# Four release points a period for held-back DMAs, W1's turned loads one user sooner, the first row squares ahead of the last gradient product

## The chip, the core and the metric

The kernel runs on one core of one Trainium2 chip. A core has five engines with an instruction stream each: TensorE (PE in the profile; weight loads are listed apart as PEld), VectorE (DVE), ScalarE (ACT), GpSimd (POOL) and SyncE (SP). Each works through its stream in order. DMAs are issued by SP, ACT or POOL, each into a queue of its own ("SPq" is SP's); 16 DMA engines move the data. A DMA whose operands are not ready makes its issuing engine wait, and all that stands behind it in that stream.

The metric is the device time of one execution in microseconds, as the median of several runs.

## The reference

One training step's forward and backward pass of a gated mix of two layers over a sequence of 2048 rows with 448 columns (bf16): a state space layer, written as a long convolution, and a dense layer with a squared ReLU.

```
def _A_ref(u, A_re, A_im, B_re, B_im, C_re, C_im, log_dt, Dskip):
    ...
    P = jnp.exp(logdA[:, :, None] * l[None, None, :])
    K = jnp.einsum("dn,dnl,dn->dl", Cc, P, dB).real
    ...                      # y = causal convolution of u with K, by FFT
    return y + u * Dskip
def _B_ref(x, w1, b1, w2, b2):
    h = jnp.einsum("bsd,df->bsf", x, w1) + b1
    r = jnp.where(h > zero, h, zero)
    return jnp.einsum("bsf,fd->bsd", r * r, w2) + b2
g = sigmoid((u * gate_w).sum(-1, keepdims=True))
out = g * a + (1 - g) * b
```

The kernel returns `out` and the gradients of `sum(out * grad_out)` by the 14 inputs other than `B_x` (the dense layer's input is `u`). Sizes: D = 448, N = 256 states, F = 1792 hidden columns, w1 448 x 1792, w2 1792 x 448.

## The kernel before

Three stages follow each other. Up to about 230 us the inputs are loaded and taken through the FFT's forward passes, and a scheduler orders the instructions. From then on the order is the program's own (`tc.manual_schedule()`, line 981): each engine runs what the Python code emits, in that sequence. This second stage, to about 625 us, interleaves two strands that have nothing to do with each other's data. From there the inverse passes and the parameter gradients close the run.

**Strand one, the convolution kernel and its gradient.** 14 chunks of 32 columns (NCH), one a period. `PERIOD` (line 1286) lists what a period does as tokens, and `token` (line 1289) carries each out. What matters here: YS puts seeds into the table Y on DVE (`seeds_y`, L1055), Y0 to Y4 build its levels on DVE (`step_y`, L1014, L1015, L1017), KM multiplies the tables on PE (`kgen`, L1078), LY issues four transposing loads of Y on SP (`load_yt`, L1102, "turned" below; they go into four tiles in R), Z0 to Z3 use these tiles on PE one period later (`back_z`, L1140), with an ACT copy each (L1146); P0 and P1 are products on DVE (L1155, L1157), S sums them on PE (L1172), X0 to X2 build the other table (L1004, L1005, L1007), FY0 to FY2 spread fields on ACT (L1040 to L1047). The seeds of the next period overwrite Y, so L1055 waits until the four turned loads have read it.

**Strand two, the dense layer.** `dense` (line 923) is a generator of small steps, and D in the list runs as many of them as their costs allow (`D_`, line 945). It consists of `first_layer`, `second_layer` and two `project` passes:

- `second_layer` (line 820) goes over 14 blocks j of 128 hidden columns. `grad_h` forms the gradient of the hidden rows on PE (L661, L664), ACT copies it into one of three tiles `dhs[j % 3]` (L784; they lie in P, F and R), `gates` multiplies it with r on DVE (L789). The function `go` then loads the r rows of block j + 3 (`load_r`, L772 or, in two halves, L775) and stores the block to `dhT_d` (L794). The block is also turned on PE (`turn`, L688, copy L689), multiplied by the input rows (`mul_2`, L697, copied out by L805), and the product turned back for storing (`turn_back`: L808, L811, L813, L814). `turn_w2` (L765, L766) prepares w2 blocks.
- `project(0, w2n)` (line 881) computes the layer's output from the squared hidden rows, `project(1, w1T)` its input gradient from `dhT_d`. Each goes over 8 row groups n of 256 rows with two halves x: 14 matmuls into a bank (L901), a copy (L904). The rows of a group come by `load_rows2(n)` (L877) into a ring of four places. In the first pass ACT squares them in place (L889): group 0 before the loop, group n + 1 while n is multiplied. After a group its place is free, and the load of group n + 4 is asked for; with it, for the first seven groups, one seventh of W1 turned (`load_w1t`, L921, a transposing load into `w1T`, which the second pass needs whole).

**Held-back DMAs.** SP's queue is in order, and the turned loads take it long. So the stores and loads above are not emitted where they are asked for. `defer` (line 633) puts them on a list `held`, and `release` (line 639) emits the list. In a period that happens at LY (behind its four loads) and at the token R, between the eighth D and FY1. Two other places force it: `force` in `hidden` and `grad_h`, where a tile is about to be reused, and a test at the head of `project`'s loop.

```
def defer(i, f):
    if hold:
        held.append((i, f))
...
elif o == "LY" and new:
    YTs[c] = [load_yt(j) for j in range(4)]
    release()
```

Of the kernel before, what the change touches and what calls it, by code (L numbers as in the profile page):

```python
# [12 lines left out]
ACT = mybir.ActivationFunctionType  # L13
# [6 lines left out]
P = 128  # L20
L, D, N, F = 2048, 448, 256, 1792
# [298 lines left out]
def kernel(ctx, tc, A_u, A_A_re, A_A_im, A_B_re, A_B_im, A_C_re, A_C_im, A_log_dt, A_Dskip,  # L320
# [4 lines left out]
    V, S, G_, T_ = nc.vector, nc.scalar, nc.gpsimd, nc.tensor  # L325
# [307 lines left out]
# [3 lines that stand above are left out]
        else:  # L636
            f()

    def release():
        while held:  # L640
            held.pop(0)[1]()
# [43 lines left out]
    def turn(j, th, src, f):  # L685
        ps = K.ps(BK["t"], [P, 8, P], bf16)
        for tt in range(8):
            T_.transpose(ps[:, tt, :], src[:, (8 * th + tt) * P:(8 * th + tt + 1) * P], ident[:])  # L688
        S.activation(hn[j % 2][:, 8 * th:8 * th + 8, :], ps[:], f)  # L689

    def mul_rows(j, th, rhs, w):
        acc[1] = th == 0
        if th == 0:
            acc[0] = K.ps(BK["a"], [P, 512])
        ps = acc[0]
        for t in range(8 * th, 8 * th + 8):
            T_.matmul(ps[:, 0:w], lhsT=hn[j % 2][:, t, :], rhs=rhs[:, t, :], start=(t == 0), stop=(t == LT - 1))  # L697
        return ps
# [14 lines left out]
    HP = FT // 2  # L713
# [47 lines left out]
    def turn_w2(j):  # L761
        ps = K.ps(BK["t"], [P, DT, P], bf16)
        for dt in range(DT):
            for h in range(1 if dt < 3 else 2):
                T_.transpose(ps[64 * h:64 * h + DSZ[dt], dt], w2b[j % 2][:, dt * P:dt * P + DSZ[dt]], ident[:], tile_position=(0, 64 * h))  # L765
        S.copy(w2T[j % 2], ps[:])  # L766
        if j + 2 < FT:
            load_w2(j + 2)

    def load_r(j):  # L770
        if j % 3 > 0:
            nc.sync.dma_start(rt[j % 3 - 1], rows_of(rT_d, j))  # L772
        else:
            for h in range(2):
                nc.sync.dma_start(r3[0][h], bass.AP(tensor=rT_d, offset=j * P * L + 1024 * h, ap=[[L, P], [1, 1024]]))  # L775

    def grad_h(j, half):

        force(j - 3)
        pss = wide(half, w2T[j % 2], lambda lb: dbt[lb])  # L780
        dh = dhs[j % 3]
        for k in range(2):
            lb = 2 * half + k
            S.mul(dh[:, 512 * lb:512 * lb + 512], pss[k][:], 2.0)  # L784

        def gate():
            force(j - 3)
            d = dh[:, 1024 * half:1024 * half + 1024]
            V.tensor_tensor(out=d, in0=d, in1=r3[j % 3][half], op=ALU.mult)  # L789
            if half == 1:  # L790
                def go():
                    if j + 3 < FT:
                        load_r(j + 3)
                    nc.sync.dma_start(rows_of(dhT_d, j), dh)  # L794
                defer(j, go)
        pend.append(gate)

    def gates():
        while pend:
            pend.pop(0)()  # L800

    def mul_2(j, th):
        ps = mul_rows(j, th, Un, D + 1)
        if th == 1:
            S.copy(dw1r[:, j % 2, 0:D + 1], ps[:, 0:D + 1])  # L805
# [14 lines left out]
    def second_layer():  # L820

        release()
        for j in range(acc.get("r", 0), 3):
            load_r(j)
        for half in range(2):
            turn_w2(half)
        for half in range(2):
            gates()
            grad_h(0, half)
            yield  # L830
        for j in range(FT):
            gates()
            if j in (3, 5, 7, 9):
                k0, k1 = (4 * (j // 2) - 4, min(4 * (j // 2), FT))
                defer(j, lambda k0=k0, k1=k1: nc.sync.dma_start(w2n[:, k0:k1], bass.AP(tensor=B_w2.tensor, offset=B_w2.offset + k0 * P * D, ap=[[D, P], [P * D, k1 - k0], [1, D]])))
            if j == FT - 1:
                load_rows2(0)
            if j + 1 < FT:
                grad_h(j + 1, 0)
            turn(j, 0, dhs[j % 3], ACT.Copy)  # L840
            yield
            if j > 0:
                mul_2(j - 1, 1)
            if j + 2 < FT:
                turn_w2(j + 2)
            yield
            gates()
            if j + 1 < FT:
                grad_h(j + 1, 1)
            turn(j, 1, dhs[j % 3], ACT.Copy)  # L850
            yield
            mul_2(j, 0)
            if j > 0:
                turn_back(j - 1)
            yield
        mul_2(FT - 1, 1)
        yield
        turn_back(FT - 1)
        load_rows2(1)
        defer(98, lambda: load_rows2(2))  # L860
        defer(99, lambda: load_rows2(3))

    PO = [0, 4, 1, 5, 2, 6, 3, 7]

    def user(n):

        return 12 if n == 15 else n - 4

    def slot_of(n):

        return pring[0 if n == 15 else n % 4]

    def load_rows2(n):
        bs = slot_of(n)
        m = FT // len(bs)
        for i, b in enumerate(bs):
            nc.sync.dma_start(b, bass.AP(tensor=rT_d if n < 8 else dhT_d, offset=256 * PO[n % 8] + i * m * P * L, ap=[[L, P], [P * L, m], [1, 256]]))  # L877
# [3 lines left out]
    def project(w, ws):  # L881

        nonlocal nbk

        def square(n, x):
            if w == 0:
                for b in slot_of(n):
                    v = b[:, :, P * x:P * x + P]
                    S.activation(v, v, ACT.Square)  # L889
        for x in range(2):  # L890
            square(0, x)
        for n in range(8):
            for x in range(2):
                t = 2 * PO[n] + x
                if any(98 <= k <= 100 + user(n + 8 * w + (w == 0 and n < 7)) for k, f in held):
                    release()
                nbk += 1
                ps = K.ps(BK["p"][nbk % len(BK["p"])], [P, 512])
                src = [b[:, j] for b in slot_of(n + 8 * w) for j in range(FT // len(slot_of(n + 8 * w)))]
                for j in range(FT):  # L900
                    T_.matmul(ps[:, 0:D], lhsT=src[j][:, P * x:P * x + P], rhs=ws[:, j, :], start=(j == 0), stop=(j == FT - 1))  # L901
                    if j == HP - 1:
                        yield
                S.copy(br[w][:, t], ps[:, 0:D])  # L904
                if n < 7:
                    square(n + 1, x)
                if x == 0:
                    gates()
                elif w == 0:
                    pend.append(lambda v=br[0][:, t - 1:t + 1]: V.tensor_tensor(out=v, in0=v, in1=b2_bc[:].unsqueeze(1).to_broadcast([P, 2, D]), op=ALU.add))  # L910
                if x == 1:
                    i = n + 8 * w
                    for m in range(4, 16):
                        if user(m) == i:
                            defer(100 + i, lambda m=m: load_rows2(m))
                    if i < HP:
                        defer(100 + i, lambda m=i: load_w1t(m))
                yield

    def load_w1t(jp):  # L920
        nc.sync.dma_start_transpose(out=w1T[:, 2 * jp:2 * jp + 2], in_=B_w1[:, 256 * jp:256 * jp + 256])  # L921
# [72 lines left out]
    X2 = 2 * W2  # L994
# [288 lines left out]
    br.extend(b[:, 0:7168].rearrange("p (t d) -> p t d", d=D) for b in (KW, DBx))  # L1283
    hold = True
    base, goal = sum(cost[0:done]), sum(cost[0:total - TAILN])
    PERIOD = """YS SA Z0 D Y0 Y1 D Z1 Y2 D Z2 Y3 D Z3 Y4 D KM KO LY WD P0 NX D P1 D X0 FY0 S X1 D R FY1 FY2 X2 D""".split()
    nd = PERIOD.count("D")

    def token(o, c):
# [50 lines left out]
    def period(c, tokens, k=0):  # L1340
        for o in tokens:
            if o == "D":
                k += 1
                D_(base + (goal - base) * (c * nd + k) // (nd * NCH - 4))
            elif c or o not in ("YS", "Y0", "Y1", "Y2", "Y3", "Y4", "LY"):
                token(o, c)
# [36 lines left out]
    for c in range(2, NCH - 1):  # L1383
        period(c, PERIOD)
    G_.dma_start(ct["F1BD"][:, 0:256], nc.inline_tensor(cs["F1K"].astype(ml_dtypes.bfloat16), name="c_F1K").ap())
    i = PERIOD.index("KM")
    praw, STs, obs = {}, {}, {}
# [19 lines left out]
    def load_sx(w, q, k, qe=nc.sync):  # L1407
        qe.dma_start(slots[k], bass.AP(tensor=sp_d[w], offset=q * 8 * D, ap=[[16 * 2 * D, P], [1, 8 * D]]))
        return slots[k].rearrange("p (a r d) -> p a r d", a=4, r=2)
# [6 lines left out]
    sx = {(0, q): load_sx(0, q, q - 1) for q in (1, 2)}  # L1416
    period(NCH - 1, [o for o in PERIOD[:i] if o != "SA"])
    D_(goal)
# [271 lines left out]
```

## Time and profile before

| | us |
|---|---|
| median of three runs (768.41, 773.26, 774.95) | 773.26 |
| the profiled execution | 771.82 |
| its span, first to last instruction | 769.9 |
| PE busy in the span | 638.2 (83%) |
| DVE busy | 566.7 (74%) |
| ACT busy | 510.9 (66%) |
| SP's queue: share of 16 DMA engines' time | 59.5% |

The views of the profile used below have these forms. A row of a timeline is start, duration, engine, line, operation, output tile <- input tiles, shape, count, and in brackets how long the engine had stood idle before it and what ended that. "SPq" rows are SP issuing DMAs: the duration is that of the issue (a merged row's includes the time between its members), not of the transfer. A row of the chain of waits is start, duration, and the engine, transfer or queue that the end of the run hung on in that time. The second view of the page cuts the span into 40 slices of 19.2 us:

```profile
PE   5958968779999888698999997998979987686666
DVE  1397586775784549598898898698879868859474
PEclk9997967899999988889999999999989998799858
```

From the eighteenth slice to the thirty-second, most of the stage with the periods, PE is busy for nine tenths of most slices and DVE for eight or nine. The seventeenth slice (308 to 327 us) is thin for both, with 6 and 5; the twenty-fifth and the thirtieth are thin for PE, with 7.

### The profile page before, as it was taken

What the parts mean: (1) busy time and instruction counts of PE and PEld (TensorE: products, weight loads), DVE (VectorE), ACT (ScalarE), POOL (GpSimd) and SP (SyncE); (2) the same over time, 40 slices, a digit from 0 to 9 for tenths busy, and PEclk for the clock granted to TensorE, in tenths of its full rate; (3) what the DMA queues carried; (4) which work ended last, traced back from release to release, by engine and by line L of the source; (5) the groups of instructions that cost most, each with busy time, mean ns of one, the idle gap of its engine ahead of it and who ended that gap; (6) DMA issues with size and microseconds to landing.
All of it is one profiled execution on the core that took longest, in us unless ns stands there. A gap on an engine that the chain in (4) does not pass through costs nothing.

```text
span 769.9 us, 20498 instructions
## 1 busy us (share of the span) xinstructions
PE 638.2 (83%) x8597; PEld 339.2 (44%) x8597; DVE 566.7 (74%) x932; ACT 510.9 (66%) x873; POOL 174.6 (23%) x296
## 2 busy tenths in 40 slices
PE   5958968779999888698999997998979987686666
PEld 2412322333456545355665654654636563433211
DVE  1397586775784549598898898698879868859474
ACT  2797958588785746477687677677725544498455
POOL 2152111112174101111211201102100332321543
PEclk9997967899999988889999999999989998799858
DMA  9898586746783995967977977999996976898995
GB/s 206 185 284 255 198 307 240 250 168 217 295 324 90 314 194 128 267 120 206 241 173 206 259 140 194 258 185 251 223 219 129 280 234 206 344 332 303 335 332 146
DMA packets 197115, 177.77 MB, mean 231 GB/s; under 512 B 121534, under 2 KB 174039, under 8 KB 196895
## 3 DMA queue, kind: packets, MB, share of 16 engines
q1 hardware_dynamic: 173823, 113.11, 59.5%
q0 software_dynamic: 15632, 44.48, 18.1%
q10 hardware_dynamic: 7568, 18.88, 6.6%
q8 instruction: 67, 1.10, 0.6%
q14 instruction: 25, 0.20, 0.1%
HBM read 83.95 MB, written 64.32 MB: 193 GB/s over the span
## 4 chain that ended last, share of the span: by engine, by line
PE 50%; ACT 15%; issue 13%; DMA 10%; DVE 7%; POOL 3%; SPq 2%; POOLq 0%; ACTq 0%; DVEq 0%
PE psN L901 9%; PE psN L661 6%; PE psN L697 5%; PE psS L1172 5%; PE psX L1078 4%; DMA U<-in_A_u_dram 3%; PE psF L1140 3%; PE psX L697 2%; PE psN L688 2%; ACT P L1146 2%; DMA hd<-F 2%; PE psN L664 2%; ACT U L689 1%; PE psN L236 1%; ACT S L1121 1%
## 5 line engine op out<-in xcount | busy, mean ns | idle before, releaser
L697 PEld LDWEIGHTS <-U 128*128 128x128 bf16 x448 | 41.5, 101 | 44.7 <-issue 15.7
L1146 ACT CAST P<-psF 128x1024 bf16<-128x1024 f32 x52 | 53.0, 1018 | 8.7 <-PE psF L1140 6.9
L1015 DVE TENSOR_TENSOR F<-Y,F 128x1024 bf16<-128x1024 bf16 (+3 forms) x70 | 47.4, 676 | 13.8 <-ACT F L1043 13.7
L1014 DVE TENSOR_TENSOR Y<-Y,F 128x1024 bf16<-128x1024 bf16 (+3 forms) x70 | 48.0, 685 | 11.1 <-ACT F L1040 7.8
L661 PEld LDWEIGHTS <-S 128*128 128x128 bf16 x336 | 30.9, 102 | 44.5 <-issue 18.7
L697 PE MATMUL psN<-S,U 128*128 128x449 bf16 x224 | 49.9, 366 | 0.0
L1017 DVE TENSOR_TENSOR Y<-Y,F 128x1024 bf16<-128x1024 bf16 (+3 forms) x70 | 48.1, 688 | 2.4
L661 PE MATMUL psN<-S 128*128 128x512 bf16 x168 | 46.3, 401 | 1.3 <-ACT U L676 1.1
L1140 PE MATMUL psF<-S,R 41*128 41x32 bf16 x1664 | 29.7, 175 | 14.1 <-ACT P L1146 12.3
L1179 POOL DMA_DIRECT2D s_d<-st x28 | 16.0, 579 | 105.1 <-ACT st L1177 87.0
L1140 PEld LDWEIGHTS <-R 41*128 41x128 bf16 x1792 | 27.5, 94 | 26.1 <-issue 23.5
L901 PEld LDWEIGHTS <-U 128*128 128x128 bf16 x252 | 24.5, 102 | 33.0 <-issue 9.8
L697 PE MATMUL psX<-D,U 128*128 128x448 bf16 x160 | 37.3, 370 | 2.0 <-ACT D L703 2.0
L689 ACT ACTIVATE U<-psN 128x1024 bf16<-128x1024 bf16 x35 | 36.2, 1033 | 0.0
L661 PE MATMUL psN<-K,S 128*128 128x512 bf16 x126 | 35.2, 410 | 0.7 <-ACT P L784 0.7
L901 PE MATMUL psN<-S,U 128*128 128x448 bf16 x140 | 30.5, 367 | 6.0 <-DMA S<-in_B_w_dram 4.7
L676 ACT ACTIVATE U<-psN,b_f 128x512 bf16<-128x512 f32 x48 | 31.1, 688 | 6.0 <-PE psN L664 4.3
L296 PEld LDWEIGHTS <-cb_MI 64*128 64x128 bf16 x256 | 15.2, 95 | 31.6 <-issue 22.3
L901 PE MATMUL psN<-D,U 128*128 128x448 bf16 x112 | 26.1, 390 | 2.7 <-ACT U L889 2.7
L1172 PEld LDWEIGHTS <-M 128*64 128x64 bf16 x896 | 25.8, 110 | 5.0 <-issue 3.1
L1172 PE MATMUL psS<-ident,P 128*64 128x128 bf16 x896 | 27.4, 219 | 0.0
L784 ACT ACTIVATE P<-psN 128x512 bf16<-128x512 f32 x20 | 10.9, 598 | 23.7 <-PE psN L664 15.2
(416 smaller groups left out, 1695.4 us busy)
## 6 DMA issues: line engine op xcount, KB each, us to landing
sp<-K ACTq DMA_DIRECT2D x8, 896.0 KB, 4.1
rT_d<-U POOLq DMA_DIRECT2D x11, 512.0 KB, 3.0
hd<-F SPq DMA_DIRECT2D x11, 448.0 KB, 14.0
U<-rT_d SPq DMA_DIRECT2D x9, 512.0 KB, 5.9
X<-gd SPq DMA_DIRECT2D x5, 896.0 KB
U<-dhT_d SPq DMA_DIRECT2D x5, 896.0 KB, 16.1
rec_d<-F ACTq DMA_DIRECT2D x2, 1920.0 KB
hd<-st ACTq DMA_DIRECT2D x8, 448.0 KB, 4.7
```

The costliest lines, as they stand in the source:

```text
L661: T_.matmul(pss[k][:], lhsT=w[:, dt], rhs=x(2 * half + k)[:, dt], start=(dt == 0), stop=False, skip_group_check=True)
L676: S.activation(r[:, 512 * lb:512 * lb + 512], pss[k][:], ACT.Relu, bias=b1_f[:, j:j + 1])
L689: S.activation(hn[j % 2][:, 8 * th:8 * th + 8, :], ps[:], f)
L697: T_.matmul(ps[:, 0:w], lhsT=hn[j % 2][:, t, :], rhs=rhs[:, t, :], start=(t == 0), stop=(t == LT - 1))
L901: T_.matmul(ps[:, 0:D], lhsT=src[j][:, P * x:P * x + P], rhs=ws[:, j, :], start=(j == 0), stop=(j == FT - 1))
L1014: V.tensor_tensor(out=run(yb, dst, [64, X2], [d0[1], n // d0[1]], [1, d0[1]]), in0=run(yb, 0, [64, X2], *src), in1=pr, op=ALU.mult)
L1015: V.tensor_tensor(out=run(vb, 0, [n, X2], [d0[1], n // d0[1]], [1, d0[1]]), in0=run(yb, 0, [64, X2], *src), in1=pi, op=ALU.mult)
L1017: return V.tensor_tensor(out=hi, in0=hi, in1=run(vb, n, [2 * n, W2], [-n, 2], [1, n]), op=ALU.add)
L1078: T_.matmul(ps[32 * g:32 * g + 32, i], lhsT=run(xb, 2048 * (1 - t) + w, [W2, 32]), rhs=Y[:, w, t, 0:NY], start=(h == 0 and t == 0), stop=( ...
L1140: T_.matmul(psz[t][:, 32 * b:32 * b + 32], lhsT=yt[64 * t:64 * t + NY, b, :], rhs=DKc[64 * t:64 * t + NY, c % 2, 16 * (j % 2) + b].rearran ...
L1146: S.copy(run(zbs[c, h][:, 0:1], 16 * (j % 2), [1024, 2], [64, NA], [32, 2], [1, 16]), run(psF[:, 0, 0:1], 0, [512, 2], [1, NA], [NA, 2], [ ...
L1172: T_.matmul(sps[64 * h:64 * h + 64, cc, r, :], lhsT=Q[h][r][:, 1024 * t + 64 * a:1024 * t + 64 * a + 64], rhs=(nident if r == 0 and t == 1 ...
```

## The change

Four edits:

- `PERIOD` has two further tokens R, behind the first and behind the third D. With LY and the old R that makes four release points a period.
- `load_w1t(0)` is asked for at the end of `second_layer`, with the rows of group 3; in `project` group i now asks for part i + 1 instead of part i, up to group 5 instead of 6.
- The squares of row group 0 are emitted in `second_layer`, before the last `mul_2` and `turn_back`; `project`'s own squares of group 0 are left out in the first pass (and did nothing in the second).
- No instruction is added or removed. The order changes on SP (from the second set of turned loads on) and for two instructions on ACT; on PE, DVE and POOL it stays.

```
@@ second_layer
             if j > 0:
                 turn_back(j - 1)
             yield
+        for x in range(2):
+            v = slot_of(0)[0][:, :, P * x:P * x + P]
+            S.activation(v, v, ACT.Square)
         mul_2(FT - 1, 1)
         yield
         turn_back(FT - 1)
         load_rows2(1)
         defer(98, lambda: load_rows2(2))
         defer(99, lambda: load_rows2(3))
+        defer(99, lambda: load_w1t(0))
@@ project
-        for x in range(2):
+        for x in range(2 * w):
             square(0, x)
...
-                    if i < HP:
-                        defer(100 + i, lambda m=i: load_w1t(m))
+                    if i < HP - 1:
+                        defer(100 + i, lambda m=i + 1: load_w1t(m))
@@ PERIOD
-YS SA Z0 D Y0 Y1 D Z1 Y2 D Z2 Y3 D Z3 Y4 D KM KO LY WD P0 NX D P1 D X0 FY0 S X1 D R FY1 FY2 X2 D
+YS SA Z0 D R Y0 Y1 D Z1 Y2 D R Z2 Y3 D Z3 Y4 D KM KO LY WD P0 NX D P1 D X0 FY0 S X1 D R FY1 FY2 X2 D
```

In SP's order this gives, for the period of the second set of turned loads (the first set has tokens of its own in a list of its own): the two halves of r for block 3 and the store of block 0 stand ahead of the four turned loads instead of behind them. In the later periods the stores and loads asked for in the first three D's of a period likewise stand ahead of its LY. Of the seven parts of W1, three stand ahead of the ninth set of turned loads (506.58 us in the profile before; one so far), three between it and the tenth (as so far), and the last behind the tenth (three so far).

More of the change, by code (lines that the diff above doesn't have):

```diff
@@ L855, in second_layer @@
             yield
+        for x in range(2):
+            v = slot_of(0)[0][:, :, P * x:P * x + P]
+            S.activation(v, v, ACT.Square)
         mul_2(FT - 1, 1)
@@ L861, in second_layer @@
         defer(99, lambda: load_rows2(3))
+        defer(99, lambda: load_w1t(0))
     PO = [0, 4, 1, 5, 2, 6, 3, 7]
@@ L889, in square @@
                     S.activation(v, v, ACT.Square)
-        for x in range(2):
+        for x in range(2 * w):
             square(0, x)
@@ L915, in project @@
                             defer(100 + i, lambda m=m: load_rows2(m))
-                    if i < HP:
-                        defer(100 + i, lambda m=i: load_w1t(m))
+                    if i < HP - 1:
+                        defer(100 + i, lambda m=i + 1: load_w1t(m))
                 yield
@@ L1285 @@
     base, goal = sum(cost[0:done]), sum(cost[0:total - TAILN])
-    PERIOD = """YS SA Z0 D Y0 Y1 D Z1 Y2 D Z2 Y3 D Z3 Y4 D KM KO LY WD P0 NX D P1 D X0 FY0 S X1 D R FY1 FY2 X2 D""".split()
+    PERIOD = """YS SA Z0 D R Y0 Y1 D Z1 Y2 D R Z2 Y3 D Z3 Y4 D KM KO LY WD P0 NX D P1 D X0 FY0 S X1 D R FY1 FY2 X2 D""".split()
     nd = PERIOD.count("D")
```

## The prediction

> **What bounds the kernel now.** I read the windows view first (busy time of each engine in stretches of 20 us, the columns being PE, weight loads, DVE, ACT, POOL, granted clock, DMA share and GB/s), then the chain of waits, then the timelines of single engines in the stage in which the change works, roughly 290 to 620 us, the periods of the hand-written order.
>
> ```profile
> 310.00:330.00 20.00, 12.61 (x205) 7.76 (x202) 11.68 (x17) 9.36 (x17) 3.65 (x7) 0.78 0.98 258
> 330.00:350.00 20.00, 20.00 (x422) 13.03 (x422) 19.01 (x26) 14.46 (x26) 1.89 (x3) 0.97 0.74 126
> ```
>
> TensorE (PE) is the engine that bounds this stage: busy for all 20.00 us of the stretch from 330 to 350. VectorE (DVE) comes second with 19.01 us there. One stretch sticks out: from 310 to 330 both fall to about 12 us, at a granted clock of 0.78. The chain of waits, the DVE and PE timelines, and the timeline of SP's queue say why:
>
> ```profile
> 302.67 12.23 SPq L1102 DMA_TRANSPOSE R<-Y  x4
> ...
> 316.88 5.85 DMA dhT_d<-P
> ...
> 286.60 0.69 DVE L789 TENSOR_TENSOR P<-P 128x1024 bf16<-128x1024 bf16 x1 [4.77 <-ACT P L784]
> 318.25 0.74 DVE L1055 COPY Y<-rec 128x256 bf16<-128x256 bf16 x1 [2.14 <-DMA R<-Y]
> 323.94 0.69 DVE L789 TENSOR_TENSOR P<-P,K 128x1024 bf16<-128x1024 bf16 x1 [4.95 <-ACT P L784]
> ...
> 324.87 0.72 PE L765 MATMUL psN<-ident,S 128*128 128x128 bf16 x5 [7.39 <-ACT U L689]
> 326.07 1.46 PE L661 MATMUL psN<-K,S 128*128 128x512 bf16 x3
> 338.43 0.82 PE L661 MATMUL psN<-K,S 128*128 128x512 bf16 x3
> ```
>
> The gradient row block 0 (tile P) is finished by the multiplication that starts at 286.60. Its store to dhT_d is held back until the four turned loads of a period (L1102, the token LY) have been issued, 302.67 + 12.23 = 314.90. It goes out at 316.88 and takes 5.85 us. Only then, at 322.7, may ACT write block 3 into the same tile; PE stands for 7.39 us behind ACT, and DVE, which works in order, for 4.95 us. Afterwards PE runs at half speed for a while: three L661 matmuls take 1.46 us instead of 0.82.
>
> **Part 1: two more release points, R after the first and third D.** No instruction is added; only the order in SP's queue moves. In the period of LY at 302.67 the store of P and the load of r for block 3 (two halves) move ahead of LY. SP has nothing else to issue there: LY waits for the last Y level anyway, so LY starts no later, and the store can go soon after 286.60 + 0.69 = 287.3, landing some 6 us later, around 294 to 296. ACT's block 3 then follows its matmuls at once.
>
> On PE this takes away 7.39 us and most of the half-speed work behind it: the six L661 matmuls alone lose 2 x (1.46 - 0.82) = 1.3 us. On DVE less goes: the 2.14 us before L1055 stay, since they hang on LY itself (its seeds overwrite what the turned loads read), and 4.95 us go. So the bounds of part 1 are 5.0 us (DVE sets the pace afterwards) and 7.39 + 1.3 = 8.7 us, or a little over 9 with the smaller matmuls behind. I take 8.5, nearer the upper end, because the next stretch is full on PE (20.00 of 20), and DVE has idle time of its own to catch up with, the next already in the following period:
>
> ```profile
> 354.49 0.38 DVE L1015 TENSOR_TENSOR F<-Y,F 128x256 bf16<-128x256 bf16 x1 [2.36 <-ACT F L1043]
> ```
>
> What is late next: the stores of blocks 1 and 2, still behind LY, leave about 2 us sooner than before since two loads and a store ahead of them are gone; their tiles are wanted only in the next period. In the other periods stores and loads of this kind caused no PE wait that I found, so moving them gains nothing; the price that they may have is the slower rival.
>
> **Part 2: the two first squares before the last mul_2.**
>
> ```profile
> 475.07 1.01 ACT L1146 CAST P<-psF 128x1024 bf16<-128x1024 f32 x1
> 476.70 0.54 ACT L805 CAST D<-psN 128x449 bf16<-128x449 f32 x1 [0.61 <-PE psN L697]
> 478.73 3.29 ACT L889 ACTIVATE U<-U 128x1792 bf16<-128x1792 bf16 x2
> ...
> 477.29 0.52 PE L811 MATMUL psN<-ident,D 128*128 128x128 bf16 x4
> 480.49 4.51 PE L901 MATMUL psN<-D,U 128*128 128x448 bf16 x14 [2.68 <-ACT U L889]
> 486.91 2.82 PE L901 MATMUL psN<-D,U 128*128 128x448 bf16 x14
> ```
>
> Before, PE waits 2.68 us for these squares. In the changed order on ACT they stand between L1146 (475.07) and L805 (476.70). ACT is idle there for only 0.61 us, so they run from about 476.1 to 479.3, and L805 moves to 479.3. But PE's L811 (turn_back, which transposes what L805 copies out) comes ahead of L901 in PE's order, and now waits for L805 until about 479.8; L901 follows at about 480.3 instead of 480.49. The wait changes its name and stays: I take 0.2 us. Bounds: -1 (L1146 behind them is 2.5 us later, and DVE with it) and 2.68 + (4.51 - 2.82) = 4.4 us, if wait and half clock went whole. [...]
>
> **Part 3: W1's turned loads one point sooner, and what that does to LY.**
>
> ```profile
> 506.58 11.36 SPq L1102 DMA_TRANSPOSE R<-Y  x4
> 518.62 3.62 SPq L921 DMA_TRANSPOSE S<-in_B_w_dram  x1
> 522.93 5.79 SPq L921 DMA_TRANSPOSE S<-in_B_w_dram  x1
> 534.89 11.96 SPq L1102 DMA_TRANSPOSE R<-Y  x4
> 564.05 13.26 SPq L1102 DMA_TRANSPOSE R<-Y  x4
> ...
> 565.97 0.91 PE L901 MATMUL psN<-S,U 128*128 128x448 bf16 x2 [3.94 <-DMA S<-in_B_w_dram]
> ```
>
> PE waits 3.94 us for the last of seven W1 loads. The SP queue is full there: a W1 load takes it 3.62 to 5.79 us. In the changed order the seventh stands one row load after the LY of 534.89, ahead of the third dhT row load. The only idle time of SP that can be won is the gap of about 3 us before 506.58; with the late store gone from this stretch as well, I put the seventh 5 to 6 us sooner, landing near 560.5, before the 562.0 (565.97 - 3.94) at which PE begins to wait. So the 3.94 us go on PE.
>
> The cost lies on LY. In front of the LY of 506.58 now stand two more W1 loads, 3.62 + 5.79 = 9.4 us, and a short row load; the 3 us gap pays for a third, and I put 1 to 2 us on the store that has left: that LY starts about 5 us later, the next, by the same account, 3 to 4 us. Behind LY wait the seeds on DVE, and behind them all of DVE's next tables:
>
> ```profile
> 521.46 0.73 DVE L1055 COPY Y<-rec 128x256 bf16<-128x256 bf16 x1
> 523.55 0.38 DVE L1015 TENSOR_TENSOR F<-Y,F 128x256 bf16<-128x256 bf16 x1 [0.92 <-ACT F L1043]
> 549.17 0.74 DVE L1055 COPY Y<-rec 128x256 bf16<-128x256 bf16 x1 [0.62 <-DMA R<-Y]
> 553.22 0.37 DVE L1015 TENSOR_TENSOR F<-Y,F 128x256 bf16<-128x256 bf16 x1 [1.78 <-ACT F L1043]
> ...
> 615.71 0.69 DVE L1017 TENSOR_TENSOR Y<-Y,F 128x1024 bf16<-128x1024 bf16 x1
> 619.43 2.27 PE L1078 MATMUL psX<-Y,R 128*32 128x41 bf16 x128
> ```
>
> After the first LY (submitted by 517.94, landing about 2 us after) the seeds at 521.46 have some 1.2 us of slack and L1015's 0.92 us behind it: 5 - 2.1 = 2.9 us of delay remain on DVE. After the second, DVE's other idle time takes up most; I carry 1 to 1.5 us of delay to the LY at 564.05. That one took 13.26 us, directly behind the last W1 load and others; freed of it, it should take about 11.4 and give back 2 us. At the end of the stage the last k-kernel product (L1078 at 619.43) needs the last Y level, 615.71 + 0.69 = 616.4. PE can therefore gain no more than 619.43 - 616.4 = 3.0 us over what DVE gains, however many waits before it vanish. I take 2.5 us for part 3, between -3 (the delay of the first LY passes whole) and 3.94 + 0.91 = 4.9 us (all of PE's wait, and the two matmuls behind it, which ran slowly, passed on whole).
>
> **The sum.** 8.5 + 0.2 + 2.5 = 11.2 us. The profiled execution took 771.82 us (span 769.9): 771.82 - 11.2 = 760.6. The three runs have a median of 773.26, which gives 762.1. I say 761.
>
> **Rivals.**
> - *The gain of part 1 stays only as far as DVE gets it (5 us), and part 3 gives nothing.* For: DVE is 19.01 of 20 busy next. Against: the 2.36 us of idle time that it can use up. 771.8 - 5 = 767.
> - *More passes through.* Parts 1 and 3 at their upper ends and half of part 2's: 8.7 + 2.2 + 4.9 = 15.8 us, 756.
> - *LY's turned loads get slower in every period.* This is the way to slower. DVE waits for LY at its seeds in five periods (the row of the waits view: 5.5 us in five waits), and what now precedes LY in the queue used to follow it.
>
> ```profile
> DVE Y L1055 <- DMA R<-Y: 5.5, 5, 2.1
> ...
> 393.42 10.02 SPq L1102 DMA_TRANSPOSE R<-Y  x4
> ...
> 407.73 0.74 DVE L1055 COPY Y<-rec 128x256 bf16<-128x256 bf16 x1 [0.87 <-DMA R<-Y]
> ```
>
> An LY with nothing in front of it took 10.02 us, the one behind a filled queue 13.26: 3.24 us more. Less the 0.92 us that L1015's wait takes up, 2.3 us in each of ten periods make 23 us, and 771.8 - 8.5 + 23 = 786. It decides from 0.85 us a period on. Against it: the LY at 534.89 stood right behind a W1 load and took 11.96, and landed 549.17 - 546.85 = 2.3 us after its last issue, while that at 393.42, with stores and loads behind it, landed 407.73 - 403.44 = 4.3 us after: what follows seems to cost more than what precedes. [...]
> - *The change does nothing where it counts*, if the store of block 0 were still behind LY. The built order on SP shows it ahead, so I give this no chance worth a number.
>
> **How the numbers follow.** About 1% (8 us) is what a measurement of this kernel can tell from no change. Chances: forecast around 761: 0.50; more passes (756): 0.15; DVE keeps it (767): 0.22; LY slower (786, or less of it): 0.13. Faster by over 1% means below 765.5: the first two and a little of the third, 0.68. Within 1%: 0.22. Slower: 0.10. For 8 in 10 the range takes in the upper ends of the terms, with 2 us of spread between runs, and the DVE case: 753 to 770.
>
> **What would show it.** Right: no wait near 7 us before L765, the store of P issued near 290, DVE's wait of 4.95 gone; PE waiting about 2.5 us at L811 instead of L901 near 470; no wait for in_B_w_dram at the start of project(1); the LY after the first W1 loads later against its Y level by some 5 us. Wrong: DVE waits of 3 us or more at L1055 in many periods, or a PE wait for rows (rT_d, dhT_d) that was not there.

## The result, and the profile after

| | before | after |
|---|---|---|
| median of 17 runs each, us | 773.26 (768.35 to 779.04) | 764.91 (760.59 to 772.13) |
| ratio, 95% interval | | 0.9903 [0.9881, 0.9925] |
| profiled execution, us | 771.82 | 767.82 |

By the ratio the change saves 7.5 us (0.97%, the interval 0.75% to 1.19%); the two medians lie 8.35 us apart. 761 was forecast, within 753 to 770. The three parts are not what the forecast made of them, as the experiments show. Lines behind 861 of the kernel before stand four further down in the changed kernel: L1055 of before is L1059, L1078 is L1082, L1102 is L1106, L901 is L905, L921 is L925.

The page's second view of the changed kernel, PE and DVE in 40 slices of 19.15 us:

```profile
PE   5958969779999876998999997987889968686666
DVE  1396586674785656898898898884898877859473
```

The seventeenth slice, thin before (6 and 5), is full for PE now, but the fifteenth and sixteenth (268 to 306 us) have become thin, with 7 and 6; in the twenty-eighth (517 to 536 us) PE stands at 7 as before, but DVE falls from 8 to 4. The timelines of SP's queue, of DVE and of PE of the changed kernel tell the first of these (the first row has three of the four turned loads of the first set):

```profile
277.69 11.66 SPq L1106 DMA_TRANSPOSE R<-Y  x3
...
292.06 0.52 SPq L794 DMA_DIRECT2D dhT_d<-P  x1
307.52 11.33 SPq L1106 DMA_TRANSPOSE R<-Y  x4
...
295.60 0.74 DVE L1059 COPY Y<-rec 128x256 bf16<-128x256 bf16 x1 [7.09 <-DMA R<-Y]
322.72 0.90 DVE L789 TENSOR_TENSOR P<-P,K 128x1024 bf16<-128x1024 bf16 x1
...
299.40 0.62 PE L688 MATMUL psN<-ident,F 128*128 128x128 bf16 x8 [2.80 <-DVE F L789]
307.51 2.05 PE L1082 MATMUL psX<-Y,X 128*32 128x41 bf16 x128 [3.81 <-DVE Y L1021]
322.10 0.50 PE L765 MATMUL psN<-ident,S 128*128 128x128 bf16 x5
323.03 0.82 PE L661 MATMUL psN<-K,S 128*128 128x512 bf16 x3
```

The store of P goes out at 292.06 and not at 316.88. The 7.39 us of PE before L765 are gone, the 4.95 us of DVE before L789 too, and three L661 behind them take 0.82 us instead of 1.46, at a granted clock of 1.00 (from 322.9 to 326.5; 0.50 from 326 to 328 before). But the seeds of this period wait 7.09 us for the first set of turned loads, and PE waits 2.80 and 3.81 us behind them. In the profile before, the seeds stood without a wait:

```profile
290.74 0.73 DVE L1055 COPY Y<-rec 128x256 bf16<-128x256 bf16 x1
```

Whether this belongs to the change is a question for more than two profiles. The table gives the ratio of each kernel's time to that of the kernel before, from many runs, and, for one profiled execution of each, the time in us from one product on PE (L1078) to a later one. The products are counted from the first one of the stage, number 0 at 236.89 before; number c belongs to chunk c. "R" are the two new release points.

| kernel | ratio | 0 to 4 | 3 to 7 | 7 to 9 | 9 to 13 | 13 to end |
|---|---|---|---|---|---|---|
| before | 1 | 131.8 | 112.5 | 56.5 | 109.7 | 150.5 |
| squares alone | 0.9976 | 131.6 | 114.0 | 56.8 | 113.0 | 149.4 |
| W1 alone | 1.0031 | 132.0 | 112.5 | 56.6 | 115.9 | 147.8 |
| R in c = 7 to 12 | 0.9958 | 131.5 | 114.0 | 54.2 | 107.4 | 151.3 |
| R in c = 2 | 0.9939 | 129.0 | 112.5 | 56.5 | 109.8 | 149.1 |
| R in c = 2, 7, 8 | 0.9962 | 126.6 | 112.5 | 55.1 | 111.6 | 151.5 |
| R in c = 2, 9 to 12 | 0.9852 | 126.6 | 112.5 | 56.6 | 108.6 | 151.1 |
| R alone, in all | 0.9848 | 126.7 | 112.5 | 55.2 | 108.0 | 148.5 |
| R and squares | 0.985 | 124.8 | 112.6 | 55.6 | 109.4 | 150.2 |
| the change | 0.9903 | 128.4 | 112.6 | 54.8 | 109.9 | 151.3 |

The first of these columns separates without overlap: 131.5 to 132.0 without R in c = 2, 124.8 to 129.0 with it (129.2 in the repeat of the change, below). It is counted from product 0 because product 1 is moved by the matmuls ahead of it: eight L697 take 1.69 us before and 3.11 with R alone, and it comes 26.5 us after product 0 in some profiles and 27.4 to 27.9 in others.

The gain in this column goes with the wait of the seeds of c = 2 for the first set. Over the ten profiles with R in c = 2, those of the kernels further below included, it is 6.9 us with R and squares, where they wait 3.92; 4.8 to 5.4 in six where they wait 4.73 to 5.29; and 2.5 to 3.4 in three where they wait 6.14 to 8.25. Product 2 is the first that needs these seeds. It comes 66.8 to 67.5 us after product 0 without R in c = 2, and 68.5 to 71.5 with it (66.8 with R and squares). So R in c = 2 makes product 2 later in most profiles and product 4 sooner in all.

The late columns scatter from one execution to the next (9 to 13 is 109.9 in the change and 114.5 in its repeat), so there the ratios of many runs decide and a profile only says which wait it was.

### The profile page after: what moved, and what is told of

The parts are those of the page before. It is cut to its first block, busy times and chain, and to the rows that moved or that the text cites. A ratio compares the mean times of both kernels' runs of the same rounds, so it can differ in the third digit from the quotient of the medians.

```text
span 766.0 us, 20505 instructions
## 1 busy us (share of the span) xinstructions
PE 633.3 (83%) x8597; PEld 339.1 (44%) x8597; DVE 566.3 (74%) x932; ACT 511.2 (67%) x873; POOL 173.4 (23%) x296
## 4 chain that ended last, share of the span: by engine, by line
PE 41%; DVE 15%; ACT 15%; issue 13%; DMA 12%; POOL 3%; SPq 1%; ACTq 0%; POOLq 0%; DVEq 0%
PE psN L661 5%; PE psN L697 5%; PE psN L905 5%; DMA R<-Y 5%; PE psS L1176 5%; PE psX L1082 4%; DVE Y L1018 3%; DVE Y L1021 3%; DVE F L1019 2%; DMA U<-in_A_u_dram 2%; DMA hd<-F 2%; PE psF L1144 1%; PE psN L688 1%; PE psX L697 1%; ACT P L1150 1%
## 5 line engine op out<-in xcount | busy, mean ns | idle before, releaser
L697 PEld LDWEIGHTS <-U 128*128 128x128 bf16 x448 | 41.0, 100 | 43.5 <-issue 14.0
L697 PE MATMUL psN<-S,U 128*128 128x449 bf16 x224 | 49.9, 366 | 0.0
L661 PEld LDWEIGHTS <-S 128*128 128x128 bf16 x336 | 30.3, 101 | 43.3 <-issue 16.7
L661 PE MATMUL psN<-S 128*128 128x512 bf16 x168 | 47.5, 410 | 0.6 <-ACT U L676 0.4
L697 PE MATMUL psX<-D,U 128*128 128x448 bf16 x160 | 37.1, 369 | 1.6 <-ACT D L703 1.6
L661 PE MATMUL psN<-K,S 128*128 128x512 bf16 x126 | 33.3, 393 | 0.7 <-ACT P L784 0.7
L905 PEld LDWEIGHTS <-U 128*128 128x128 bf16 x252 | 23.7, 99 | 21.9 <-issue 1.8
L1059 DVE COPY Y<-rec 128x256 bf16<-128x256 bf16 x14 | 10.4, 740 | 25.0 <-DMA R<-Y 23.1
L905 PE MATMUL psN<-S,U 128*128 128x448 bf16 x140 | 28.4, 353 | 0.0
L1176 PEld LDWEIGHTS <-P 128*64 128x64 bf16 x896 | 26.0, 110 | 0.8 <-issue 0.7
```

The source lines that it names most:

```text
L661: T_.matmul(pss[k][:], lhsT=w[:, dt], rhs=x(2 * half + k)[:, dt], start=(dt == 0), stop=False, skip_group_check=True)
L1176: T_.matmul(sps[64 * h:64 * h + 64, cc, r, :], lhsT=Q[h][r][:, 1024 * t + 64 * a:1024 * t + 64 * a + 64], rhs=(nident if r == 0 and t == 1 ...
```

## The experiments

**The three parts one by one.** First, the kernel before with the two R in `PERIOD` and nothing else:

```
-PERIOD = """YS SA Z0 D Y0 Y1 D Z1 Y2 D Z2 Y3 ...
+PERIOD = """YS SA Z0 D R Y0 Y1 D Z1 Y2 D R Z2 Y3 ...
```

> The kernel before with the two new release points alone (no squares moved, W1 as before). Theory A (what the profile after shows is typical): the 7.4 us wait behind the store of block 0 goes, but the first set of turned loads lands some 5 us later because two loads and a store now stand right behind it, so the product of period 3 is only 3 to 4 us earlier than before: ratio 0.995. Theory B (the late landing in the profile after is chance): 7 to 9 us, ratio 0.990, and the seeds of period 2 wait under 2 us.

Measured: 763.11 us, 0.9848 [0.9816, 0.9879], 11.8 us off. The release points alone do more than the whole change. Neither theory had it: the gain lies beyond B's, and yet the seeds of period 2 wait, as in A:

```profile
293.53 0.74 DVE L1055 COPY Y<-rec 128x256 bf16<-128x256 bf16 x1 [5.25 <-DMA R<-Y]
```

Second, the two squares moved and nothing else:

```
+        for x in range(2):
+            v = slot_of(0)[0][:, :, P * x:P * x + P]
+            S.activation(v, v, ACT.Square)
         mul_2(FT - 1, 1)
...
-        for x in range(2):
+        for x in range(2 * w):
             square(0, x)
```

> The kernel before with the two first squares moved alone. Theory A (the shift of 2 us at the product of the period around 480 us in the profile after comes from them): PE's wait moves to L811 and is about as long, but the 14 matmuls behind run at full speed, 1.5 to 2.5 us in all, of which little may reach the end: ratio 0.997 to 1.000. As predicted (0.2 us): ratio 1.000.

Measured: 772.14 us, 0.9976 [0.9951, 1.0002], 1.9 us off if anything. The timeline of PE of this kernel (its L904 is L901 before) shows the next wait:

```profile
499.15 1.12 PE L904 MATMUL psN<-D,S 128*128 128x448 bf16 x5 [2.93 <-ACT S L892]
```

The squares of a later row group, waited for by 0.3 us before, now come 2.93 us late. Third, W1's seven parts one user sooner and nothing else:

```
         defer(99, lambda: load_rows2(3))
+        defer(99, lambda: load_w1t(0))
...
-                    if i < HP:
-                        defer(100 + i, lambda m=i: load_w1t(m))
+                    if i < HP - 1:
+                        defer(100 + i, lambda m=i + 1: load_w1t(m))
```

> The kernel before with W1's parts one user sooner alone (release points as before). Theory A: the wait for the last part of 3.9 us goes, and the seeds of a later period wait longer for the turned loads behind the W1 parts, 0 to 5 us: ratio 0.995 to 1.000. Rival: the delay of the turned loads outweighs it: ratio above 1.000.

Measured: 776.03 us, 1.0031 [1.0011, 1.0051], 2.4 us slower: the rival. In its profile the ninth set takes 11.21 us and the seeds behind it wait 0.98. PE's wait for W1 is gone, but for rows of dhT that go out behind the twelfth set PE now waits 4.14 us (1.35 before), and the fourteen matmuls behind take 4.50 us (2.82 before; its L902 is L901):

```profile
616.49 4.50 PE L902 MATMUL psN<-S,U 128*128 128x448 bf16 x14 [4.14 <-DMA U<-dhT_d]
```

The parts alone come to -11.8 - 1.9 + 2.4 = -11.3 us, the change to -7.5.

**The release points but not W1.** The changed kernel with W1 as before:

```
-        defer(99, lambda: load_w1t(0))
...
-                    if i < HP - 1:
-                        defer(100 + i, lambda m=i + 1: load_w1t(m))
+                    if i < HP:
+                        defer(100 + i, lambda m=i: load_w1t(m))
```

> The changed kernel with W1's parts asked for as before. Theory W (W1's parts one user sooner cost time; they put a third part ahead of the ninth set of turned loads): about the sum of the two parts alone, 11.8 + 1.9 us, ratio 0.982 to 0.985. Rival (W1 sooner pays when the release points are there): slower than the changed kernel, ratio above 0.992.

Measured: 761.54 us, 0.985 [0.9806, 0.9894]: level with the release points alone, and 4 us below the change (whose interval begins at 0.9881, so that these two overlap a little; that of the release points alone, ending at 0.9879, just does not). So W1 sooner costs about as much beside the release points as it does alone, or a little more, and the squares add nothing that can be told beside them.

**Where the release points act.** The first of these takes the first R out of period c = 2 of the changed kernel:

```
-        period(c, PERIOD)
+        period(c, PERIOD if c > 2 else PERIOD[:4] + PERIOD[5:])
```

> The changed kernel without the first new release point in period 2, so that the loads of block 3 and the store of block 0 leave after the third step group, some 8 us behind the first set of turned loads instead of right behind it, and still ahead of the second set. Theory A: the seeds of period 2 wait under 2 us instead of 7, the product of period 2 is back at its old time, and 3 to 4 us are won over the changed kernel: ratio to before 0.985 to 0.987. Theory B (chance): as the changed kernel, 0.990.

Measured: 767.52 us, 0.9907 [0.9871, 0.9942]. It turned out to be a repeat of the change: the order on SP is the same, since the point that was left out had nothing in the list that the next one doesn't release ahead of the same load. Its use is as a second profile: the seeds behind the ninth set of turned loads wait 11.3 us in it, 9.10 in the first, so that wait is no accident of one execution.

The kernel before with the two R in period c = 2 only, where `PERIOD_R` is the list with the two R and `PERIOD_BEFORE` that without:

```
-        period(c, PERIOD)
+        period(c, PERIOD_R if c == 2 else PERIOD_BEFORE)
```

> The kernel before with the two new release points in period 2 alone. Theory P1 (what the release points bring is the store of block 0 ahead of the second set): most of the 11.8 us, ratio 0.985 to 0.989, the 7.4 us wait gone. Rival P2 (half of it comes from the other periods, the last ones above all): ratio 0.991 to 0.995.

Measured: 768.93 us, 0.9939 [0.9908, 0.997]: 4.7 us of the 11.8. Then the same in other periods, c = 7 to 12 and c = 2, 7, 8:

```
-        period(c, PERIOD)
+        period(c, PERIOD_BEFORE if c < 7 else PERIOD_R)
...
+        period(c, PERIOD_BEFORE if c not in (2, 7, 8) else PERIOD_R)
```

> The kernel before, with the two new release points in the periods from the eighth chunk on only (c = 7 to 12), none in c = 2 to 6; W1 and squares as before. Known so far: the release points everywhere give 0.985 (11.8 us), those of period 2 alone 0.994 (4.7 us), so 7 us have come from elsewhere. Late theory: they come from the stretch after 440 us, in which the DMA engines are full: the last store of dhT (490 us before, 458 with the release points) and the first row loads of project(0) go out sooner, so the ratio is 0.990 to 0.992 (7 us off) here, although the stall of 7.4 us before L765 is back. Middle theory: the gain comes from periods 3 to 6, whose loads of r and stores go sooner too: 0.998 to 1.002 here. Chance theory: the difference of 7 us is spread between runs: anything from 0.993 to 1.0.

> The kernel before, with the two new release points in three periods, c = 2, 7 and 8. If the late gain comes from the last stores of dhT and the first row loads of project(0) alone, this has all of the gain of the release points: 0.984 to 0.987 (10 to 12 us off). If it comes from c = 9 on, where row loads and W1 loads go ahead of the turned loads, it has no more than period 2 alone: 0.993 to 0.995. If it comes from c = 3 to 6: the same 0.993 to 0.995, and the run with c = 7 to 12 then shows nothing.

Measured: 770.79 us, 0.9958 [0.9924, 0.9992] for c = 7 to 12, and 770.12 us, 0.9962 [0.9929, 0.9996] for c = 2, 7 and 8. The periods c = 7 to 12 alone bring 3.2 us (0.6 to 5.9), less than the late theory's 7 and in the range of the chance theory. The store of block 13 and the first row loads, which c = 7 and 8 send out sooner, add nothing to c = 2 that can be told. The DMA engines, which the late theory has full after 440 us, had in the kernel before a share of 0.76 from there to 460, 0.80 to 480 and 1.14 from 480 to 570. What is left are c = 9 to 12, tried together with c = 2:

```
+        period(c, PERIOD_BEFORE if c in range(3, 9) else PERIOD_R)
```

> The kernel before, with the two new release points in c = 2 and in c = 9 to 12, none in c = 3 to 8. Known: everywhere 0.985; c = 2 alone 0.994; c = 7 to 12 alone 0.996; c = 2, 7 and 8 together 0.996. If the release points of c = 3 to 8 do nothing (the profiles show the same pace of 112.5 us from the fifth product to the ninth with and without them), this has all of the gain: 0.984 to 0.988. If they have a part of their own in it that one profile doesn't show: 0.990 (the product of the parts) to 0.993.

Measured: 763.26 us, 0.9852 [0.9814, 0.9891]. Release points in c = 2 and in c = 9 to 12 have all of the gain. (The pace that the expectation names is the column "3 to 7".) The wait that goes there is found in the timelines of SP and PE, first of the kernel before, then of this one:

```profile
591.43 11.32 SPq L1102 DMA_TRANSPOSE R<-Y  x4
602.81 0.57 SPq L877 DMA_DIRECT2D U<-dhT_d  x1
...
609.57 2.82 PE L901 MATMUL psN<-S,U 128*128 128x448 bf16 x14 [1.35 <-DMA U<-dhT_d]
```

```profile
572.22 2.61 SPq L877 DMA_DIRECT2D U<-dhT_d  x2
580.98 0.36 SPq L877 DMA_DIRECT2D S<-dhT_d  x1
585.25 12.19 SPq L1102 DMA_TRANSPOSE R<-Y  x4
```

Before, a row group that `project(1)` needs is loaded behind a set of turned loads, and PE waits for it. With release points it is issued 10 us ahead of that set. PE's wait for U<-dhT_d is in the profile of every kernel without R in these periods (1.35, 2.39, 1.74, 3.15 and, with W1 alone, 4.14 us) and in none with them. Behind the two longest of these waits the fourteen matmuls also take longer (4.51 and 4.50 instead of 2.82 us). That is a gain of 1.4 to 5.8 us by the profiles. The runs give 773.26 x (0.9939 - 0.9852) = 6.7 us beside c = 2, with an interval of some 4 us to either side, and 3.2 us where c = 7 to 12 stand alone. The rest, if it is real, isn't shown by any one profile.

**Why W1 sooner costs.** The waits of the changed kernel around the ninth set of turned loads, on SP, DVE and PE:

```profile
490.76 3.07 SPq L925 DMA_TRANSPOSE S<-in_B_w_dram  x1
493.94 0.52 SPq L881 DMA_DIRECT2D U<-rT_d  x1
494.50 7.78 SPq L925 DMA_TRANSPOSE S<-in_B_w_dram  x1
502.40 0.51 SPq L881 DMA_DIRECT2D U<-rT_d  x1
502.95 3.26 SPq L925 DMA_TRANSPOSE S<-in_B_w_dram  x1
506.31 15.96 SPq L1106 DMA_TRANSPOSE R<-Y  x4
...
501.54 0.42 DVE L1129 TENSOR_TENSOR S<-S,vw 128x512 bf16<-128x512 bf16 x1
527.05 0.73 DVE L1059 COPY Y<-rec 128x256 bf16<-128x256 bf16 x1 [9.10 <-DMA R<-Y]
...
538.36 2.06 PE L1082 MATMUL psX<-Y,X 128*32 128x41 bf16 x128 [3.26 <-DVE Y L1021]
```

The last Y level is done at 501.54, where L1129 follows it; the turned loads start 4.8 us later and take 15.96 us (11.36 before). DVE stands for 9.10 us, and PE for 3.26 behind it. The DMA engines are full there, in the windows view (columns as in the prediction):

```profile
510.00:530.00 20.00, 17.64 (x256) 10.26 (x256) 9.19 (x15) 14.18 (x17) 3.29 (x5) 0.91 1.20 202
530.00:550.00 20.00, 15.55 (x358) 10.43 (x359) 19.41 (x27) 10.67 (x13) 1.29 (x3) 0.91 1.20 217
```

DMA share stands at 1.20 in both (1.17 and 1.18 in the kernel before), DVE at 9.19 of 20 in the first (17.30 before). Three experiments put the parts of W1 elsewhere. The changed kernel with the third part left out:

```
+                    if i < HP - 1 and i != 1:
```

> The changed kernel with the third of W1's seven turned loads left out (one seventh of the weights of the input gradient is then not loaded). Theory W: only two parts stand ahead of the ninth set, the seeds behind it wait under 3 us instead of 9, the product of that period comes 4 to 5 us earlier, and the whole is near the kernel without W1's shift: ratio 0.982 to 0.986. Rival (the queue is full anyway, the place of one part makes no difference): ratio 0.989 to 0.991, seeds waiting 7 us or more.

Measured: 765.14 us, 0.9897 [0.9856, 0.9938]. A miss: the ninth set took 16.75 us with two parts ahead of it, and the time didn't move. The third part alone is not the cost. With that part loaded one user later instead (two parts ahead of the ninth set, four between it and the tenth):

```
+                    for m in {0: (1,), 2: (2, 3), 3: (4,), 4: (5,), 5: (6,)}.get(i, ()):
+                        defer(100 + i, lambda m=m: load_w1t(m))
```

> The changed kernel with the third W1 part asked for one user later, so that two parts stand ahead of the ninth set of turned loads, four ahead of the tenth and one behind. Theory W: the wait moves from the seeds behind the ninth set to those behind the tenth and is no shorter: ratio 0.988 to 0.993. Rival (only the ninth set is tight, the tenth has slack): as without the shift, 0.982 to 0.986.

Measured: 764.22 us, 0.9891 [0.9849, 0.9932]. Nothing again that can be told. The wait is shared out: the ninth set takes 14.75 us and the tenth 14.41, and the seeds behind them wait 4.09 and 5.58. Last, parts 0 and 1 as before the change, and only the later ones sooner:

```
-        defer(99, lambda: load_w1t(0))
...
+                    for m in {0: (0,), 1: (1,), 2: (2, 3), 3: (4,), 4: (5,), 5: (6,)}.get(i, ()):
+                        defer(100 + i, lambda m=m: load_w1t(m))
```

> The changed kernel, but with parts 0 and 1 of W1 asked for where the kernel before asks for them, and only parts 3 to 6 one user sooner: two parts ahead of the ninth set of turned loads (as with W1 untouched), four between the ninth and the tenth, one behind. Order theory: what costs time is that a row load of 0.9 MB stands right in front of the ninth set because W1's first parts were put ahead of it; the ninth set then takes 12 to 13 us as with W1 untouched (15 to 17 us with W1 sooner), and since PE no longer waits 4 to 5 us for the last part at the start of project(1), the ratio is 0.980 to 0.985 (761.5 us and less). Rival: any W1 part moved ahead of a set of turned loads costs what it takes, because the DMA engines are full from 480 to 570 us; the tenth set gets slower (15 us and more, 14 with W1 untouched), DVE's seeds behind it wait longer, and the ratio is 0.988 to 0.991, as for the whole change.

Measured: 763.92 us, 0.988 [0.9841, 0.9919]. The ninth set is short again (12.72 us), as the first theory has it, but the tenth takes 15.35, as the second has it, and the time is no better than with W1 as before. Here the profiles show why so little can be won. First the release points alone, PE and DVE:

```profile
557.65 0.90 PE L901 MATMUL psN<-S,U 128*128 128x448 bf16 x2 [4.20 <-DMA S<-in_B_w_dram]
561.45 1.76 PE L1078 MATMUL psX<-Y,R 128*32 128x41 bf16 x108
...
548.68 0.74 DVE L1055 COPY Y<-rec 128x256 bf16<-128x256 bf16 x1 [8.93 <-DMA R<-Y]
559.68 0.69 DVE L1017 TENSOR_TENSOR Y<-Y,F 128x1024 bf16<-128x1024 bf16 x1
```

Then the kernel with the later parts sooner (its L904, L1081, L1058, L1020 and L1105 are L901, L1078, L1055, L1017 and L1102):

```profile
531.37 15.35 SPq L1105 DMA_TRANSPOSE R<-Y  x4
...
553.44 0.54 PE L904 MATMUL psN<-S,U 128*128 128x448 bf16 x2 [0.94 <-DMA S<-in_B_w_dram]
560.70 2.05 PE L1081 MATMUL psX<-Y,R 128*32 128x41 bf16 x128 [4.79 <-DVE Y L1020]
...
548.95 0.74 DVE L1058 COPY Y<-rec 128x256 bf16<-128x256 bf16 x1 [8.54 <-DMA R<-Y]
559.95 0.69 DVE L1020 TENSOR_TENSOR Y<-Y,F 128x1024 bf16<-128x1024 bf16 x1
```

In both, the last Y level of this period is done at 560.4 to 560.6, because the seeds wait for the tenth set of turned loads until 548.7 to 549. PE's product needs that level. With W1 late, PE waits 4.20 us for W1 and comes to the product at 561.45, 1.1 us after the level; with W1 early it arrives sooner and waits 4.79 us for the level. One wait takes the place of the other, and 1.1 us is all that could be won there (2.2 in the profile of R and squares). In the profile before, the product comes 6.6 us after its level: the release points have used that room up.

## Why the prediction was right

The direction and the range were right and the time 4 us low, by errors that partly cancel: part 1 was worth more than its term, part 3 had the wrong sign. That the sum comes so near is in part luck. The saving of 0.97% also lies just short of the 1% that the prediction gave 0.68 to pass, and its interval reaches to both sides of that line.

**Part 1, 8.5 us forecast.** In its own place the mechanism held: the store at 292.06, no wait at L765, DVE's 4.95 us gone. The size there was too large. R in c = 2 alone give 4.7 us (2.3 to 7.1), and the stage up to product 4 gains 4.8 to 5.4 us in six of ten profiles and 3.4 in that of the change: about the lower bound of 5.0, which the prediction had set for DVE. The step that failed is "DVE has idle time of its own to catch up with", and with it a term that was put at nothing. "LY starts no later" was asked of the second set of turned loads. But the store and the two halves of r now go out right behind the first set, and the seeds of the same period hang on that one: they wait 7.09 us in the changed kernel and 5.25 with the release points alone, and product 2 comes 1.7 to 4.7 us later than before in all profiles with R in c = 2 but one. That these three transfers hold up the first set is argued, for no run moved them alone. The seeds can wait without them too (4.41 us with W1 alone, 3.96 with the squares alone), but product 2 is not late there.

The second failure is a sentence: "In the other periods stores and loads of this kind caused no PE wait that I found, so moving them gains nothing". There was one, 1.35 us for U<-dhT_d at 609.57, and from c = 9 on the release points bring some 7 us beside those of c = 2. Together that makes up the 11.8 of the release points alone.

**Part 2, 0.2 us forecast.** The wait changed its name as foretold. ACT and PE of the changed kernel:

```profile
472.63 3.29 ACT L858 ACTIVATE U<-U 128x1792 bf16<-128x1792 bf16 x2
475.81 0.53 ACT L805 CAST D<-psN 128x449 bf16<-128x449 f32 x1
...
476.39 0.52 PE L811 MATMUL psN<-ident,D 128*128 128x128 bf16 x4 [2.57 <-ACT D L805]
476.84 2.82 PE L905 MATMUL psN<-D,U 128*128 128x448 bf16 x14
```

PE waits 2.57 us at L811 instead of 2.68 at L901. The term left out that the fourteen matmuls behind can take 2.82 us (at a granted clock of 1.00) instead of 4.51 (at a mean of 0.62). Whether they do varies: with the squares moved they do so in four of seven profiles (4.04 to 4.38 us in the others), and with the squares in their old place in one of seven. The 1.9 us that the runs give have an interval that takes in nothing, and the wait for later squares (2.93 us) stands against more.

**Part 3, 2.5 us forecast as a gain; 2.4 us lost alone, about 4 beside the release points.** The ninth set started 4.8 us behind its Y level as against "about 5 us", and PE's wait for W1 is gone; both were foretold. In the changed kernel two steps failed. The set also takes 4.6 us longer, which the sum left out for it, so that the delay on DVE was not the 2.9 us that it carried but a wait of 9.10. And the cap on PE's gain was looked for at the last product (3.0 us at 619.43), not at the first product behind the wait, at 561: there, once the release points have taken DVE's slack, it is 1.1 us. With W1 alone the first of these does not show (11.21 us for the set, 0.98 us for the seeds); the loss there goes with PE's 4.14 us for U<-dhT_d. A reading was narrow, too: the seven W1 loads before hold SP for 3.23 to 6.26 us, not 3.62 to 5.79.

**The rivals.** "DVE keeps it" is nearest in time (767 for 764.91) and names the right engine; its 5 us for part 1 agree with the 4.7 of c = 2 alone, its nothing for part 3 is still too kind. "LY slower" happens at the ninth set but not in every period: two seeds of twelve wait 3 us or more, 7.09 and 9.10. Against it the prediction leaned on two rows by which what follows a set costs more than what precedes it. The ninth set does not bear that out: it took 11.36 us with one W1 part ahead, 12.58 with two in the release points alone, 15.96 with three. But with two parts ahead it also took 11.21 us (W1 alone) and 16.75 (the third part left out), so the count alone doesn't settle it.

**The best of what was run** are the release points without the earlier W1: alone 0.9848 [0.9816, 0.9879], with the squares 0.985 [0.9806, 0.9894], in c = 2 and 9 to 12 only 0.9852 [0.9814, 0.9891].

**Open.** Whether the late release points bring 7 us, as beside c = 2, or less, and by which waits, where the profiles show 1.4 to 5.8; and which step makes W1 sooner cost about 4 us beside the release points. The three kernels with its parts elsewhere (0.988 to 0.9897) can't be told from the change (0.9903), nor, with six runs each, clearly from the kernel with W1 as before (0.985).

## What to carry to other kernels

Before a wait for a transfer is paid for with earlier queue places, look at the next thing that the waiting engine needs: if that is ready 1 us before the engine comes, 1 us is what can be won. In a stretch where the DMA engines are full (a share of 1.20 here), a load moved forward can move another back: the ninth and tenth sets took 15.96 and 11.44 us in the changed kernel, 12.72 and 15.35 with only the later parts of W1 sooner. So let those go first whose reader holds up what else its engine has to do, as the seeds did on DVE for 9.10 us. And a wait that is missing from one profile may be in the next: compare several before a term is set to zero.

## What the runs showed of the hardware

How fast the matmuls behind a wait run does not follow from the wait's length alone. Ahead of the first fourteen L901 PE waits 2.68 us in all seven profiles with the squares in their old place. In six of them the fourteen then take 4.49 to 4.51 us; in the seventh, R in c = 7 to 12, they take 2.82:

```profile
478.85 2.82 PE L901 MATMUL psN<-D,U 128*128 128x448 bf16 x14 [2.68 <-ACT U L889]
```

The windows view of the wait and of the fourteen matmuls in the kernel before, and of the fourteen behind the wait of 2.57 us in the changed kernel:

```profile
477.81:480.49 2.68, 0.00 (x1) 0.01 (x1) 2.52 (x3) 2.68 (x6) 1.29 (x2) 1.00 1.30 107
480.49:485.00 4.51, 4.51 (x18) 1.78 (x22) 1.50 (x2) 1.53 (x1) 0.00 (x0) 0.62 1.07 262
```

```profile
476.84:479.66 2.82, 2.82 (x19) 1.35 (x22) 2.27 (x2) 1.02 (x4) 1.29 (x2) 1.00 1.09 232
```

The granted clock is 1.00 during the wait before and 0.62 on average over the matmuls behind it; in the changed kernel it is 1.00 over these. Behind a longer wait, 2.93 us with the squares alone, seven matmuls of the same shape take 1.50 us, as seven behind 0.30 us do before. What decides between the two is not shown.

Four turned loads of the same size, from the second set on, held SP for 10.0 to 16.8 us in these profiles (10.02 at 393.42 in the kernel before, 16.75 for the ninth set without the third part of W1). What sets the length is not shown.
